# One visit of the attention products instead of two in the gated stage of an mLSTM cell with a SwiGLU block

## The chip, the cores and the metric

The kernel runs on one core of one Trainium2 chip. The metric is the device time of one execution in microseconds (us). The engines are TensorE (PE; its weight loads are shown apart as PEld), VectorE (DVE), ScalarE (ACT), GpSimd (POOL) and SyncE (SP, which here only issues DMA transfers). Each engine works through its own queue in order and waits for the others by semaphores.

## The reference

Two blocks follow one another. The first is an mLSTM cell over 4 batches, 8 heads, 768 positions and 40 features per head (float32): a decaying matrix state per head, with exponential gates, a normaliser and an output gate.

```python
m_new = np.maximum(f_gate[:, :, t] + m, i_gate[:, :, t])
f_stab, i_stab = np.exp(f_gate[:, :, t] + m - m_new), np.exp(i_gate[:, :, t] - m_new)
C = f_stab * C + i_stab * outer(v_t, k_t)        # (40 x 40) per head
n = f_stab * n + i_stab * k_t
y_t = sigmoid(o_gate_t) * (C @ q_t) / max(|n . q_t|, 1)
```

The result, as a matrix x of 3072 tokens by 320 features, goes through `(silu(x @ w_gate) * (x @ w_val)) @ w_out` with an inner width of 1536. The output is 3072 by 320.

## The kernel before, in words

The 768 positions are cut into six groups of 128 (`NG`), and each group into two halves of 64. The cell is computed group by group in the form of attention: within a half, scores of q and k (`sp`) times weights from the gates (`w_sb`) times v, and from the state at the start of the half, q times the state `C`. The 32 heads of all batches are dealt with in two sets P = 0 and 1 of 16 heads each.

The feed-forward block works on one group (512 tokens) at a time: `hidden` and `project_all` for group 0, and for the groups g = 1 to 5 the stage `gated` (products with w_gate and w_val) and then `project_seven` (product with w_out). While group g is in `gated`, the cell of the next group n = g + 1 is computed in between, and the data of group f = g + 2 is loaded. So attention products stand in the gated stages of g = 1 to 4.

`gated` runs over k = 0 to 5. In each step TensorE computes, on PSUM tiles `gv_x` (X) and `gv_y` (Y), two banks each: the first products of X (copied by ACT, L932, into a room `uw` in `tmp` or `x_sb`), the last product of the step before into its Y (`second(k-1)`), the first products of Y, and the second products of X, which are added to the same PSUM tile as the first. DVE adds Y to the room (L942), and X to a second room `c12` (L951); ACT takes the Silu of X (L950) and of `c12` (L952), DVE (L953) and POOL (L955) multiply. `second` is followed by L920 on DVE, L922 on ACT, L923 and the sums L790 to L792 on POOL.

Four places in each step are called "a" (after the first products of X), "b" (after `second`), "c" (after the first products of Y) and "d" (at the end). The dictionary `at`, filled near the end of the file, says by hand which functions are called at which place and step; their instructions enter each engine's queue in exactly that order. Nothing is reordered afterwards. The PSUM of this part is a list `pairs` of four pairs of banks: `take` removes the pair at the front, `give` and `pairs.append` put one back at the end, and the first write to a pair waits for what read it before.

The attention of one set P consists of: `attend_inter` (L433, q times the state) and `attend_intra` (L442, weights times v), 32 products each on TensorE, which the profile shows as 64 records; `gather` on DVE, which multiplies the first by the decay (L451, twice), adds the second (L455, four times), and makes the divisor `den` (L458 to L460); `gate` on POOL (L465), which multiplies the output gate `o_sb` by `den`; and `divide` on DVE (L471, twice), which writes x into the space of `k_sb` (`x_all`). From there `send_squares` (L484) moves x in blocks of 32 by 32 into `x_sq`, where `turn_inputs` (L488, on DVE, in `project_seven`) reads it. `loads_behind` issues the transfers of v (L139) and of the weights (L515) for group f, which overwrite what the intra products read.

Of the kernel before, what the change touches and what calls it, by code (L numbers as in the profile page):

```python
# [24 lines left out]
def kernel(  # L25
# [18 lines left out]
    nc = tc.nc  # L44
    B, H, S, D = q.shape
    BH = B * H
    NG = S // L
# [5 lines left out]
    DM, DF = moe_w_gate.shape  # L53
# [3 lines left out]
    SQ = 32  # L57
    NKC = DM // HP
# [35 lines left out]
    def give(name, P):  # L94
        if held:
            pairs.append(held[name].pop(0))

    def half(i):
        return slice(i * SUB, (i + 1) * SUB)
# [5 lines left out]
    def heads(P):  # L105
        return slice(P * UH, (P + 1) * UH)
# [6 lines left out]
    vw_sb = const.tile([128, BH, D1], F32)  # L113
# [14 lines left out]
    x_sq = const.tile([128, B * NKC, L // SQ, SQ], F32)  # L128
# [168 lines left out]
    for u in range(B):  # L297
        r = slice(u * BH, (u + 1) * BH)
        for P in range(2):
            a = u * BH + P * UH + u * HQ  # L300
# [142 lines left out]
                                 start=True, stop=True)  # L443
        return intra

    def gather(n, P, inter, intra):
        y = vw_sb[:, heads(P)]
        y2 = y.rearrange("p (a two) d -> p two a d", two=2)
        e2 = e_T[:, n, heads(P)].rearrange("p (a two) -> p two a", two=2)
        for two in range(2):  # L450
            nc.vector.tensor_tensor(y2[:, two], inter[two], e2[:, two].unsqueeze(2).to_broadcast([128, UA, D1]), op=ALU.mult)  # L451
        give("inter", P)
        for i, c in QUAD:
            t = y2[half(i), i ^ c]
            nc.vector.tensor_tensor(t, t, intra[i][half(c)], op=ALU.add)  # L455
        give("intra", P)
        den = work.tile([128, UH, 1], F32, name="den")
        nc.vector.scalar_tensor_tensor(den, in0=y[:, :, D:], scalar=-1.0, in1=y[:, :, D:], op0=ALU.mult, op1=ALU.max)  # L458
        nc.vector.tensor_scalar(den, den, scalar1=1.0, scalar2=None, op0=ALU.max)
        nc.vector.reciprocal(den, den)  # L460
        return y, den
# [15 lines left out]

    x_all = k_sb.rearrange("p h d -> p (h d)")[:, 0:B * DM]

    def send_squares(P):  # L480
        for t in range(L // SQ):
            src = x_all[t * SQ:(t + 1) * SQ, 2 * P * DM:(2 * P + 2) * DM].rearrange("p (w e) -> p w e", e=2 * SQ)
            for r in range(2):
                nc.sync.dma_start(out=x_sq[r * SQ:(r + 1) * SQ, 2 * P * NKC:(2 * P + 2) * NKC, t, :],  # L484
                                  in_=src[:, :, r * SQ:(r + 1) * SQ])

    def turn_inputs(n, u):
        nc.vector.transpose(out=xT(n)[half(0), :, ts(u, L)],  # L488
# [470 lines left out]
    live = {}  # L959
# [8 lines left out]
    def do_add(n, pairs_of=(0, 1)):  # L968
        for P in pairs_of:
            live["add", P] = add(n, P)  # L970
# [18 lines left out]
    def do_intra(P):  # L989
        live["intra", P] = attend_intra(P)  # L990

    def do_attend(n, P):
        do_inter(n, P)
        do_intra(P)

    def do_gather(n, P, then=True):
        live["y", P] = gather(n, P, live.pop(("inter", P)), live.pop(("intra", P)))
        if then:
            do_gate(P)

    def do_gate(P):
        gate(P, live["y", P][1], nc.gpsimd)
# [4 lines left out]
    def load_all(dst, a, n, eng=nc.sync):  # L1007
        for P in range(2):
            load(dst, a, n, P, eng)

    run = lambda f, *a, **b: (lambda: f(*a, **b))
# [15 lines left out]
        9: [run(do_weigh, 0), run(do_weigh, 1), run(do_decayed, 2)],  # L1027
        10: [run(do_add, 1, (0,)), run(rounded, 12), run(load_squares, q_sq, q, 2, (0,))],
        11: [run(do_intra, 0), run(do_inter, 1, 0), run(do_gather, 1, 0, False), run(piece_load, 10),
             run(load_squares, q_sq, q, 2, (1,))],  # L1030
    }
# [7 lines left out]
    def early_squares(part):  # L1039
# [7 lines left out]
    after = {  # L1047
        0: [run(do_inter, 1, 1), run(convert, 14), run(sig, 0), run(sig, 1), run(do_gate, 0)],
        1: [run(do_intra, 1), run(do_gather, 1, 1), run(weights_load, 2), run(load_all, v_sb, v, 2), run(load_all, k_sb, k, 2)],
        2: [run(do_divide, 1, 0), run(convert, 15), run(early_squares, 0)],  # L1050
        3: [run(do_divide, 1, 1), run(weights_cap, 0)],
# [20 lines left out]
    def loads_behind(f):  # L1072
        return [run(load_all, v_sb, v, f), run(weights_load, f)]

    def between(g):
        n, f = g + 1, g + 2
        at = {i: [] for i in range(8)}
        if f < NG:
            at[0] += [run(load_squares, q_sq, q, f)]
        if n < NG:  # L1080
            at[0] += [run(turn_inputs, n, u) for u in range(B)]
            at[1] += [run(double_inputs, n, u) for u in range(2)]
        if f < NG:
            at[2] += [run(weights_cap, 0), run(weights_cap, 1)]
            if g == 1:
                at[1] = [run(out_weights, V, 2)] + at[1]
            at[3] += [run(weights_bias, f, 0), run(weigh_values, G, 0), run(weights_bias, f, 1), run(weigh_values, G, 1)]
            at[4] += [run(sig, 0), run(sig, 1), run(turn_squares, q_sq, qT)]
        if n < NG:
            at[4] += [run(input_sums, V)]  # L1090
        if f < NG:
            at[6] += [run(do_decayed, 2 * f)]
        return at

    for g in range(1, NG):
        n, f = g + 1, g + 2
        at = {}
        if n < NG:
            at["a", 0] = []
            if g > 1:  # L1100
                do_add(n)
                at["a", 0] = [run(do_state, 2 * n)]
            at["b", 1] = [run(do_scores), run(do_weigh, 0), run(do_weigh, 1)]
            at["b", 2] = [run(do_attend, n, 0), run(do_gather, n, 0)]
            at["d", 2] = [run(do_divide, n, 0), run(send_squares, 0)]
            at["b", 3] = [run(do_attend, n, 1), run(do_gather, n, 1)]
            at["d", 3] = [run(do_divide, n, 1), run(send_squares, 1)]
        if f < NG:
            at["a", 0] += [run(load_squares, k_sq, k, f)] + ([run(load_all, o_sb, o_gate, 2)] if g == 1 else [])
            at["c", 1] = [run(turn_squares, k_sq, kT)]  # L1110
            at["b", 3] += loads_behind(f)
            at["d", 3] += [run(load_all, o_sb, o_gate, f)]
            at["b", 4] = [run(load_all, k_sb, k, f)]
        if g == 1:
            at["b", 4] = at.get(("b", 4), []) + [run(out_weights, V, 0)]
            at["d", 4] = [run(out_weights, V, 3)]
            at["c", 5] = [run(out_weights, V, 1)]
            at["b", 2] = [run(sig, 0), run(sig, 1)] + at["b", 2]
            for j, w, e, parts in ((1, ("b", 0), G, (0, 1)), (2, ("c", 0), G, (0, 1)), (3, ("d", 0), V, (0,)), (3, ("c", 1), V, (1,)),
                                   (4, ("c", 2), G, (0, 1)), (5, ("a", 4), V, (0, 1))):  # L1120
                at[w] = [run(weight_sums, j, e, parts)] + at.get(w, [])
        gated(g, at)
        project_seven(g, between(g))
# [30 lines left out]
```

## Time and profile before

| what | value |
|---|---|
| median of 3 runs | 517.11 us (509.97, 519.29, 517.11) |
| the profiled execution | 509.04 us, span 507.2 us |
| granted TensorE clock | 1.000 |
| TensorE busy | 501.3 us, 99% of the span |
| DVE, ACT, POOL busy | 332.8, 208.2, 260.2 us |
| gated stages g = 1 to 4, with attention | 53.5 us each (from 123.2, 201.1, 279.0 and 357.0 us) |
| gated stage g = 5, without attention | 46.8 us (from 433.5 us) |
| inter products L433, all | 640 records, 11.7 us |
| intra products L442, all | 640 records, 11.3 us |
| x_sq<-k_sb transfers | 64 of 40 KB, 3.0 us to landing |

The page gives for each group of instructions the line of the kernel, the engine, the operation, the tiles written and read, the busy time, the mean of one instruction and the idle time of the engine ahead of it. The chain that ended last is followed back from the last instruction, at each step to what released it. A timeline has the start and the length of merged instructions of one engine in order; in brackets stands how long the engine was idle before and what released it. Matmuls overlap in the pipeline, so the difference of two starts says more about the cost of a block than the length of one record.

### The profile page before, as it was taken

Reading aid. Unit: us, or ns where it says so; the run is one execution under the profiler, and the core shown is the slowest. Engines: PE = TensorE matmul, PEld = TensorE weight load, DVE = VectorE, ACT = ScalarE, POOL = GpSimd, SP = SyncE. Lnnn points to the kernel's source line nnn. Section 1 sums busy time; section 2 is a strip of 40 time slices with the busy share of each in tenths; the row PEclk is TensorE's granted clock in tenths of the full one; section 3 lists DMA queues with packets and bytes.
Section 4 is the critical chain, followed back from the end, with each engine's and each line's share of the span. In section 5 each row is a group of like instructions: output and inputs, shape, how many; then the busy total and the mean of one; then the engine's idle time right before and its main releaser. Section 6 shows DMA issues by size and latency. Waiting matters only on the chain.

```text
span 507.2 us, 15081 instructions
## 1 busy us (share of the span) xinstructions
PE 501.3 (99%) x6437; PEld 425.8 (84%) x6437; DVE 332.8 (66%) x543; ACT 208.2 (41%) x404; POOL 260.2 (51%) x292
## 2 busy tenths in 40 slices
PE   8999999999999999999999999999999999999997
PEld 4855555767998899888899888899888899988896
DVE  5889668889998677578375677477568454233421
ACT  3675774467252356323248312339321330223200
POOL 3744433358877834466634357643357650176710
PEclk9999999999999999999999999999999999999999
DMA  9999998696705991403992503991101100000001
GB/s 147 190 250 224 170 225 181 142 178 109 105 5 89 164 92 55 55 1 61 172 107 41 74 3 52 163 126 20 42 3 25 31 2 27 27 1 1 0 14 39
DMA packets 184746, 43.29 MB, mean 85 GB/s; under 512 B 173000, under 2 KB 180184, under 8 KB 184040
## 3 DMA queue, kind: packets, MB, share of 16 engines
q1 hardware_dynamic: 183284, 38.26, 47.6%
q0 software_dynamic: 1264, 4.02, 3.2%
q8 instruction: 50, 0.82, 0.7%
q14 instruction: 16, 0.13, 0.1%
q10 hardware_dynamic: 132, 0.07, 0.0%
HBM read 35.68 MB, written 4.01 MB: 78 GB/s over the span
## 4 chain that ended last, share of the span: by engine, by line
PE 92%; DMA 3%; SPq 2%; ACT 1%; DVE 1%; issue 0%; DVEq 0%; ACTq 0%
PE gv_x L902 26%; PE o_ps L823 23%; PE gv_y L902 21%; PE o_ps L769 5%; PE gv_ps L752 5%; PE inter L433 2%; PE sp L384 2%; DMA raw<-in_moe_w_val_dram 2%; PE intra L442 2%; PE add L410 2%; DMA M_dram<-M_sb 1%; SPq L139 1%; ACT h_sb L583 1%; PE sp L600 1%; PE burn L546 1%; PE tp_x L507 1%
## 5 line engine op out<-in xcount | busy, mean ns | idle before, releaser
L902 PE MATMUL gv_x<-xT,wgv_sb 64*128 64x256 f32 x720 | 89.1, 377 | 0.0
L902 PEld LDWEIGHTS gv_x<-xT,wgv_sb 64*128 64x128 f32 x720 | 69.6, 187 | 7.9 <-issue 0.2
L823 PE MATMUL o_ps<-wo_sb,h_sb 128*128 128x160 f32 x480 | 67.4, 300 | 0.0
L823 PEld LDWEIGHTS o_ps<-wo_sb,h_sb 128*128 128x128 f32 x480 | 65.6, 190 | 1.7 <-issue 1.7
L950 ACT ACTIVATE h_sb<-gv_x 128x256 f32<-128x256 f32 x30 | 11.5, 383 | 116.3 <-PE gv_x L902 116.3
L752 PE MATMUL gv_ps<-xT,wgv_sb 64*128 64x512 f32 x240 | 53.7, 595 | 0.1
L752 PEld LDWEIGHTS gv_ps<-xT,wgv_sb 64*128 64x128 f32 x240 | 25.6, 187 | 23.1 <-issue 20.3
L902 PE MATMUL gv_y<-xT,wgv_sb 64*128 64x256 f32 x360 | 43.9, 376 | 0.0
L902 PE MATMUL gv_y<-q_sb,wgv_sb 64*128 64x256 f32 x360 | 43.9, 376 | 0.0
L395 POOL TENSOR_TENSOR vw_sb<-v_sb,w_sb 128x656 f32<-128x656 f32 x10 | 13.9, 1389 | 49.9 <-ACT w_sb L534 38.1
L902 PEld LDWEIGHTS gv_y<-xT,wgv_sb 64*128 64x128 f32 x360 | 35.0, 187 | 3.9
L902 PEld LDWEIGHTS gv_y<-q_sb,wgv_sb 64*128 64x128 f32 x360 | 35.0, 187 | 3.9
L823 PE MATMUL o_ps<-wT,S 128*128 128x160 f32 x240 | 33.4, 299 | 0.0
L823 PEld LDWEIGHTS o_ps<-wT,S 128*128 128x128 f32 x240 | 32.9, 190 | 0.0
L534 ACT ACTIVATE w_sb<-w_sb,g_T 128x64 f32<-128x64 f32 x128 | 31.0, 336 | 0.0
L902 PE MATMUL gv_x<-q_sb,sw 64*128 64x256 f32 x240 | 30.9, 376 | 0.0
L943 POOL TENSOR_TENSOR tmp<-tmp 128x512 f32<-128x512 f32 x15 | 20.0, 1332 | 16.8 <-DVE tmp L942 16.8
L923 POOL TENSOR_TENSOR h_sb<-x_sb 128x512 f32<-128x512 f32 x12 | 15.7, 1311 | 24.6 <-ACT x_sb L922 24.6
L923 POOL TENSOR_TENSOR h_sb<-tmp 128x512 f32<-128x512 f32 x13 | 16.5, 1269 | 21.5 <-ACT tmp L922 21.5
L769 PE MATMUL o_ps<-wo_sb,h_sb 128*128 128x320 f32 x96 | 27.4, 439 | 0.0
L790 POOL TENSOR_TENSOR S<-h_sb 128x256 f32<-128x256 f32 x30 | 22.6, 754 | 9.2 <-DVE h_sb L923 7.3
L942 DVE TENSOR_TENSOR tmp<-tmp,gv_y 128x1024 f32<-128x1024 f32 x15 | 18.1, 1205 | 13.8 <-PE gv_y L902 12.0
(226 smaller groups left out, 993.4 us busy)
## 6 DMA issues: line engine op xcount, KB each, us to landing
w_sb<-M_dram SPq DMA_DIRECT2D x10, 512.0 KB, 6.7
v_sb<-in_v_dram SPq DMA_DIRECT2D x12, 320.0 KB, 6.2
o_sb<-in_o_gate_dram SPq DMA_DIRECT2D x12, 320.0 KB, 5.9
raw<-in_moe_w_out_dram SPq DMA_DIRECT2D x3, 1280.0 KB, 7.1
k_sb<-in_k_dram SPq DMA_DIRECT2D x10, 320.0 KB, 7.6
x_sq<-k_sb SPq DMA_DIRECT2D x64, 40.0 KB, 3.0
q_sb<-in_q_dram SPq DMA_DIRECT2D x32, 64.0 KB, 3.7
raw<-in_moe_w_gate_dram SPq DMA_DIRECT2D x3, 640.0 KB
```

Source lines behind the costliest of these rows:

```text
L384: nc.tensor.matmul(sp[two][half(i), a, :], lhsT=kT[feats(two), P * UA + a, half(i)], rhs=qT[feats(two), P * UA + a, half(i)], start=True, ...
L395: eng.tensor_tensor(vw_sb[:, heads(P)], v_sb[:, heads(P)], w_sb[:, heads(P), last].to_broadcast([128, UH, D1]), op=ALU.mult)
L534: nc.scalar.activation(w_sb[:, h], w_sb[:, h], AF.Exp, bias=g_T[:, n, h:h + 1], scale=-1.0)
L752: nc.tensor.matmul(ps[i], lhsT=wgv_sb[half(i), m, kc, :], rhs=x[half(i), kc, :], start=(kc == 0), stop=(kc == NKC - 1))
L769: nc.tensor.matmul(ps[u], lhsT=hid(g, m)[:, ts(u, L)], rhs=wo_sb[:, m, :], start=(m == 0), stop=(m == NFC - 1))
L790: eng.tensor_tensor(S1[:, k], lo[:, second_half], hi[:, second_half], op=ALU.add)
L823: nc.tensor.matmul(node[x][:, i], lhsT=lhs(k)[:, ts(i, L)], rhs=rhs(k), start=start and k == 0 and i == 0, stop=stop and k == KH - 1, skip ...
L902: nc.tensor.matmul(ps[:, i, cols], lhsT=lhs(c)[half(i)], rhs=rhs(c)[half(i)], start=start and c == 0, stop=stop and c == n - 1, skip_group ...
L923: (nc.vector if k == KH - 1 else nc.gpsimd).tensor_tensor(h_sb[:, 2 * k + 1], uw[:, 0], uw[:, 1], op=ALU.mult)
L942: nc.vector.tensor_tensor(uw, uw, y, op=ALU.add)
L943: nc.gpsimd.tensor_tensor(uw[:, :, second_half], uw[:, :, second_half], uw[:, :, first_half], op=ALU.add)
L950: nc.scalar.activation(h[:, first_half], x[:, 0, first_half], AF.Silu)
```

## The change

Before, the inter and intra products of set 0 stood at place "b" of k = 2, and those of set 1 at place "b" of k = 3, each followed by its gather on DVE; set 0 was divided and sent at "d" of k = 2, set 1 at "d" of k = 3. Now the inter products of both sets and then the intra products of both follow one another at "b" of k = 2. The first part of `gather`, the multiplication by the decay, is a function of its own (`scaled`) and is called for both sets between the inter and the intra products, and gives their PSUM pairs back. Gather 0 follows at "b" of k = 2, gather 1 and divide 0 at "c" of k = 2, divide 1 at "d" of k = 2. After it `send_squares` moves both sets in one series: 8 transfers of 80 KB instead of 16 of 40 KB. `loads_behind` moves from "b" of k = 3 to "d" of k = 2, ahead of divide 1 and the transfers. On POOL the gate of set 1 now stands ahead of L955 and the sums of k = 2. Each engine issues the same computing instructions as before.

```diff
-    def gather(n, P, inter, intra):
+    def scaled(n, P, inter):
...
+    def gather(n, P, intra):
...
-    def send_squares(P):
+    def send_squares():
         for t in range(L // SQ):
-            src = x_all[t * SQ:(t + 1) * SQ, 2 * P * DM:(2 * P + 2) * DM].rearrange("p (w e) -> p w e", e=2 * SQ)
+            src = x_all[t * SQ:(t + 1) * SQ].rearrange("p (w e) -> p w e", e=2 * SQ)
             for r in range(2):
-                nc.sync.dma_start(out=x_sq[r * SQ:(r + 1) * SQ, 2 * P * NKC:(2 * P + 2) * NKC, t, :],
-                                  in_=src[:, :, r * SQ:(r + 1) * SQ])
+                nc.sync.dma_start(out=x_sq[r * SQ:(r + 1) * SQ, :, t, :], in_=src[:, :, r * SQ:(r + 1) * SQ])
...
+    def do_scaled(n, P):
+        scaled(n, P, live.pop(("inter", P)))
...
-            at["b", 2] = [run(do_attend, n, 0), run(do_gather, n, 0)]
-            at["d", 2] = [run(do_divide, n, 0), run(send_squares, 0)]
-            at["b", 3] = [run(do_attend, n, 1), run(do_gather, n, 1)]
-            at["d", 3] = [run(do_divide, n, 1), run(send_squares, 1)]
+            at["b", 2] = [run(do_inter, n, 0), run(do_inter, n, 1), run(do_scaled, n, 0), run(do_scaled, n, 1),
+                          run(do_intra, 0), run(do_intra, 1), run(do_gather, n, 0)]
+            at["c", 2] = [run(do_gather, n, 1), run(do_divide, n, 0)]
+            at["d", 2] = (loads_behind(f) if f < NG else []) + [run(do_divide, n, 1), run(send_squares)]
+            at["d", 3] = []
...
-            at["b", 3] += loads_behind(f)
```

More of the change, by code (lines that the diff above doesn't have):

```diff
@@ L444, in attend_intra @@
         return intra
-    def gather(n, P, inter, intra):
-        y = vw_sb[:, heads(P)]
-        y2 = y.rearrange("p (a two) d -> p two a d", two=2)
+    def scaled(n, P, inter):
+        y2 = vw_sb[:, heads(P)].rearrange("p (a two) d -> p two a d", two=2)
         e2 = e_T[:, n, heads(P)].rearrange("p (a two) -> p two a", two=2)
@@ L452, in gather @@
         give("inter", P)
+    def gather(n, P, intra):
+        y = vw_sb[:, heads(P)]
+        y2 = y.rearrange("p (a two) d -> p two a d", two=2)
         for i, c in QUAD:
@@ L994, in do_attend @@
         do_intra(P)
+    def do_scaled(n, P):
+        scaled(n, P, live.pop(("inter", P)))
     def do_gather(n, P, then=True):
-        live["y", P] = gather(n, P, live.pop(("inter", P)), live.pop(("intra", P)))
+        if ("inter", P) in live:
+            do_scaled(n, P)
+        live["y", P] = gather(n, P, live.pop(("intra", P)))
         if then:
```

## The prediction

> **What bounds the kernel now.** I read the page from the top (busy shares, then the chain that ended last), then the chain in order of time for one stage, then the timeline of each engine in that stretch.
>
> ```profile
> PE 501.3 (99%) x6437; PEld 425.8 (84%) x6437; DVE 332.8 (66%) x543; ACT 208.2 (41%) x404; POOL 260.2 (51%) x292
> ...
> PE 92%; DMA 3%; SPq 2%; ACT 1%; DVE 1%; issue 0%; DVEq 0%; ACTq 0%
> ```
>
> TensorE works all the time and is 92% of the chain; nearly all of the other 8% lies before 90 us, where the change does nothing. The chain in the stage g=2, around both visits of the attention products:
>
> ```profile
> 219.59 1.29 PE gv_y L902 x12
> 220.89 1.07 PE inter L433 x64
> 221.96 0.93 PE intra L442 x64
> 222.90 2.36 PE gv_y L902 x20
> 225.25 4.32 PE gv_x L902 x40
> ...
> 239.55 3.45 PE gv_y L902 x32
> 243.00 4.32 PE gv_x L902 x40
> ```
>
> Every piece starts where the one before ends: no engine makes TensorE wait here, and the stages g=1, 3 and 4 look the same. So only two things can move the end: TensorE's own work, and a new wait of TensorE. DVE (33 to 46 us busy of each 53.5 us stage) has slack on average; what counts is where its queue is late.
>
> **The change, part by part.** Let T be the start of the first inter product, by the timeline 220.82 us in g=2 (142.93, 298.72 and 376.70 in the others).
>
> *TensorE.* A half-step without attention is 3.45 of gv_y; with a visit it is 1.29 + 1.07 + 0.93 + 2.36 = 5.65, so a visit costs 2.20 us. By the starts in the timeline that is 0.95 from inter to intra, 0.95 for intra, and about 0.30 for the changes of kind (gv_y's twelve take 1.40 instead of 1.29 up to inter, intra takes 1.05 up to gv_y, the next eight 0.97 instead of 0.87). The same 256 records are issued per stage, but one visit goes. Two visits are 4.40; one long one is 4 x 0.95 + 0.30 = 4.10. **Gain 0.30 us per stage, 1.2 us in four stages** (0.8 to 1.4: two inter blocks in a row are not in this trace; the bounds are 0.2 and 0.35 by the two ways of reading the changes).
>
> *New wait for PSUM.* The pool has four pairs and X of k=2 holds one. inter 0, inter 1 and intra 0 take the other three, so intra 1 gets inter 0's pair and must wait for the two DVE multiplications that now stand first, and the next gv_y gets inter 1's. Inter 0 ends about T+1.1; L451 starts at T+1.21 (222.03) and two take 0.91, so that pair is free at T+2.12, and intra 1 wants it at T+2.85. The second pair is free at T+3.07 (two more, 0.93 apart), and gv_y wants it at T+3.90. Both have 0.7 to 0.8 us to spare, in g=1 too, where DVE came late from its transposes and still began L451 at T+1.21 (144.14). Cost nothing; each us that DVE is later than T+1.9 would cost one.
>
> *New order on DVE.* This is the step that I expect to cost. Gather 1 and divide 0 used to stand in the next half-step; now they stand ahead of L951 of k=2. Behind L951 stands, on ACT, the Silu L952, and behind that the copy L932 of k=3's first products, which TensorE must see finished before it adds the second products to the same pair. The rows of before:
>
> ```profile
> 222.03 0.91 DVE L451 TENSOR_TENSOR vw_sb<-inter,e_T 128x328 f32<-128x328 f32 x2 [0.35 <-PE inter L433]
> 222.96 2.02 DVE L455 TENSOR_TENSOR vw_sb<-vw_sb,intra 64x328 f32<-64x328 f32 x4
> 225.01 0.33 DVE L458 SCALAR_TENSOR_TENSOR den<-vw_sb 128x16 f32<-128x16 f32 x1
> ...
> 226.22 1.16 DVE L942 TENSOR_TENSOR x_sb<-x_sb,gv_y 128x1024 f32<-128x1024 f32 x1
> 228.31 0.69 DVE L951 TENSOR_TENSOR x_sb<-x_sb,gv_x 128x512 f32<-128x512 f32 x1 [0.92 <-ACT h_sb L950]
> ...
> 229.24 1.44 DVE L471 TENSOR_TENSOR k_sb<-o_sb,vw_sb 128x320 f32<-128x320 f32 x2
> ```
> ```profile
> 229.03 0.42 ACT L952 ACTIVATE x_sb<-x_sb 128x256 f32<-128x256 f32 x1 [0.76 <-DVE x_sb L951]
> 229.67 1.01 ACT L932 COPY tmp<-gv_x 128x1024 f32<-128x1024 f32 x1 [0.23 <-PE gv_x L902]
> 231.69 0.63 ACT L922 ACTIVATE x_sb<-x_sb 128x512 f32<-128x512 f32 x1 [1.01 <-DVE x_sb L920]
> ```
>
> In before that copy ends at 230.68 and TensorE needs it at 235.06 (second gv_x products of k=3): 4.4 us of cover. After, DVE goes: four L451 to T+3.07; four additions of gather 0 (intra 0 lands about T+3.1) 2.05, to T+5.17; den 1.21, to T+6.38; L942 waits for gv_y (T+3.90+0.97+1.30, and 0.26 until it is seen) and starts at T+6.43, 1.14 to T+7.57; gather 1 2.05 + 1.21, to T+10.83; divide 0, d; then 0.72 from L951 to L952, 0.33 from L952 to the copy (219.49 to 219.81 in k=1), 1.00 of copy, 0.06 to be seen. The copy is done at T+12.94+d. TensorE arrives at the second products at 235.06 - 220.82 - 0.30 = T+13.94. **Stall = d - 1.0.** L471's single durations run from 484 to 1039 ns, so d for two lies between 0.9 and 2.1. In before the pair took 1.44 beside 0.81 us of Pool. Now it begins together with Pool's gate 1 (L465, 1262 ns): 0.9 free, plus 0.54 x 1.26/0.81 = 0.84, gives d = 1.75, near the upper rows; in g=1 Pool's weight sums lie there instead, and the pair beside them took 1.80. Stall 0.75 per stage, 3.0 in four; the ends are 0 and 1.1.
>
> [...]
>
> What is late next: divide 1 follows L953 and ends by T+15.4, L920 of k=2 by T+16.1, L942 of k=3 by T+17.3; TensorE asks for these at T+19 or later, so they stay covered, by about 2 us. Pool reaches L943 of k=3 some 3 us later than now, which delays a DVE instruction and no product.
>
> *Transfers.* Sixteen sends of 40 KB (a batch of eight keeps SP's queue 6.5 to 7.9 us, 3.0 us to landing) become eight of 80 KB, and the loads of v and w move ahead of them, from T+17 to T+4 or so. One new send takes between one old issue (0.84) and two; eight take 7 to 14 us from T+15.4, so they are issued by g=2's 243 to 250, against 249.05 now. Their reader, L488, runs at 257.01. Behind them the loads of o and k come no later, and those of q, free only when gv_y's last use of q_sb ends at 254.66, begin at 255.57 now and at most 0.9 earlier. Gain and loss nothing: everything lies under TensorE.
>
> **Sum.** 4 x (0.75 - 0.30) = **+1.8 us** on the profiled execution (span 507.2, time 509.04): 510.8. The ends are -1.2 (no stall) and +3.6 (stall 1.1, gain 0.2). The other three executions shown took 509.97, 517.11 and 519.29, on which a change of this size is lost; the mean of the four is 513.85, and with 1.8 I forecast **515.7 us**, 1.4 below the median of the runs with nothing added.
>
> **Rivals.**
> 1. No stall: DVE finishes divide 0 within 1.0 us, as the shortest L471 rows would have it, and only the saved visit is left: -1.2 us, 512.7. For it: TensorE waited for nothing in the stages; against it: Pool's gate starts in the same moment.
> 2. Slower by over 2%, through the same place: TensorE stands in k=3 before its second gv_x products because the copy is late. Price: each us beyond d = 1.0 costs 4 us over the stages, and 2% (10.2 us) is passed at d = 3.85, that is, if the DVE and ACT chain of 10.6 us from T+2.2 ran about a fifth longer than its rows. A stall of 2.85 in each stage gives 524.1 on the mean. For it: the whole 4.4 us of cover is spent and nothing is left to absorb a miss; against: the chain's rows repeat within 0.1 us in three stages.
> 3. The transfers don't do what they seem to: 640 short rows of one send land so late that L488 waits. They would have to land after 257, some 7 to 14 us after their issue, against 3.0 (at most 7.4) now; a delay of 3 us per stage shifts TensorE only when input sums come after 279, and they end at 274.7. Time as forecast, 516.
>
> **How the numbers follow.** Forecast with a stall 0.55; no stall 0.25; slower through the stall 0.10; transfers 0.02; the rest, 0.08, is scatter between executions, since 509 to 519 is itself 2%, and 2% is about what a measurement of this kernel can tell from no change. I split it 0.05 faster, 0.03 slower. Faster 0.05, same 0.82, slower 0.13. Range: 509.04 - 1.2 = 507.8 to 519.29 + 3.6 = 522.9, so 508 to 523; it leaves out the second rival and some scatter.
>
> **What would show it.** In the profile after: inter x128 and intra x128 in one block per stage, some 4.1 us long with its changes; no idle time before intra; L932 of k=3 ending near T+14.7, and TensorE idle 0.4 to 1.1 us before the second gv_x products of k=3, released by ACT. Wrong if TensorE waits instead before intra 1 or gv_y (the PSUM pairs), if the wait in k=3 is over 2 us, or if L488 waits for a transfer.

## The result and the profile after

| what | before | after |
|---|---|---|
| median, 22 runs each, side by side | 511.19 us (508.91 to 520.17) | 518.53 us (513.91 to 526.58) |
| ratio | | 1.0121, 95% interval 1.0098 to 1.0143 |
| the profiled execution, span | 509.04 us, 507.2 | 518.4 us, 516.6 |
| start of the state products (`add`, L410) of groups 1 to 4 | 121.66, 199.71, 277.60, 355.50 | 123.86, 206.30, 285.81, 364.76 |
| from one to the next (g=1, g=2, g=3) | 78.05, 77.89, 77.90 | 82.44, 79.51, 78.95 |
| from the fourth to the end of the span (g=4, g=5) | 151.70 | 151.84 |

The kernel got 1.2% slower, 6.2 us, where +1.8 was forecast. The ratio leaves out the slow executions (five of after's 22, from 522.54 us up), so it lies below the ratio of the two medians, which are 7.3 us apart. Lines of the new kernel have slightly higher numbers in what follows: the copy L932 is L934, L942 is L944, L951 to L955 are L953 to L957, L465 is L468 and L471 is L474. The last three rows of the table cut the span at a point that every kernel of this study has; a period holds one gated stage and the product with w_out behind it. The spans differ by 9.4 us: 2.20 before group 1, where the change does nothing (that stretch varies from execution to execution, as the table of the experiments shows), then 4.39, 1.62 and 1.05 in the stages g=1, 2 and 3, and 0.14 in all that follows.

The page's busy shares and the shares of the chain, after:

```profile
PE 505.1 (98%) x6437; PEld 426.6 (83%) x6437; DVE 335.9 (65%) x543; ACT 208.1 (40%) x404; POOL 266.3 (52%) x292
...
PE 87%; DVE 4%; DMA 3%; ACT 2%; issue 2%; SPq 1%; DVEq 0%; ACTq 0%
```

The number of products is the same, TensorE's busy time grew by 3.8 us only, and its share of the chain fell from 92 to 87%. "issue", time in which an engine waited for nothing that the profile shows, rose from 0 to 2% of the chain. The chain of the stage g=2 in order of time (start, length, what) shows where:

```profile
226.18 1.29 PE gv_y L904 x12
227.47 2.01 PE inter L433 x128
229.48 1.28 PE intra L442 x87
230.75 1.43 issue
232.18 0.83 PE intra L442 x41
233.01 2.36 PE gv_y L904 x20
...
243.16 4.59 PE gv_x L904 x40
```

In the middle of the intra products TensorE stands still for 1.43 us. No engine releases it, and the place is not record 64, where the products of the second set, with inputs and a PSUM pair of their own, begin: it is record 87 of 128. The other stages have the same, at other places (timeline of TensorE; in brackets the idle time before the piece and its releaser):

```profile
147.30 1.10 PE L442 MATMUL intra<-v_sb,w_sb 64*64 64x41 f32 x58
150.19 1.93 PE L442 MATMUL intra<-v_sb,w_sb 64*64 64x41 f32 x70 [1.78 <-issue]
...
308.80 1.93 PE L442 MATMUL intra<-v_sb,w_sb 64*64 64x41 f32 x116
311.55 0.43 PE L442 MATMUL intra<-v_sb,w_sb 64*64 64x41 f32 x12 [0.82 <-issue]
...
387.85 2.33 PE L442 MATMUL intra<-v_sb,w_sb 64*64 64x41 f32 x128
```

The idle time lies behind record 58, 87 and 116 of intra in g=1, 2 and 3, each time 29 records further. In g=4 nothing is cut off, but 128 records that otherwise take 2.08 take 2.33. Before has no idle time in any of its eight visits of 64 + 64 records.

Two smaller things appear besides. In the last row of the chain the second products of X in k=3 take 4.59 instead of 4.32: that is the forecast wait for the copy, and it comes back below. And the windows of g=1 (length, busy time and number of instructions of each engine, then the granted clock, the DMA share and GB/s) show a slow clock:

```profile
144.90:150.10 5.20, 3.24 (x188) 2.96 (x186) 3.58 (x8) 4.14 (x6) 2.83 (x4) 1.00 0.02 5
150.50:153.90 3.40, 3.40 (x73) 2.99 (x69) 2.59 (x7) 1.26 (x1) 1.42 (x3) 0.50 0.56 98
154.00:163.00 9.00, 9.00 (x86) 7.74 (x82) 7.12 (x13) 1.10 (x3) 6.74 (x8) 1.00 0.73 156
```

Right behind the 1.78 us of idle time TensorE had half its clock for 3.4 us, which costs 1.7 us of work. With it g=1 adds up: 1.78 idle, 1.7 clock, 0.50 before the copy, 0.27 before the second inter block, less 0.30 for the saved visit, is 3.95 of 4.39 (1.7 is an estimate, half of 3.4).

### The profile page after: what moved, and what is told of

Its sections match the earlier page's. It is cut to its first block, busy times and chain, and to the rows that moved or that the text cites. A ratio compares the mean times of both kernels' runs of the same rounds, so it can differ in the third digit from the quotient of the medians.

```text
span 516.6 us, 15035 instructions
## 1 busy us (share of the span) xinstructions
PE 505.1 (98%) x6437; PEld 426.6 (83%) x6437; DVE 335.9 (65%) x543; ACT 208.1 (40%) x404; POOL 266.3 (52%) x292
## 4 chain that ended last, share of the span: by engine, by line
PE 87%; DVE 4%; DMA 3%; ACT 2%; issue 2%; SPq 1%; DVEq 0%; ACTq 0%
PE gv_x L904 23%; PE o_ps L825 22%; PE gv_y L904 19%; PE gv_ps L754 7%; PE o_ps L771 5%; DMA raw<-in_moe_w_gate_dram 3%; PE intra L442 2%; PE inter L433 2%; PE add L410 2%; PE sp L384 1%; ACT h_sb L585 1%; DMA o_sb<-in_o_gate_dram 1%; SPq L368 1%; PE tp_x L509 1%; PE sp L602 1%
## 5 line engine op out<-in xcount | busy, mean ns | idle before, releaser
L944 DVE TENSOR_TENSOR tmp<-tmp,gv_y 128x1024 f32<-128x1024 f32 x15 | 18.3, 1219 | 16.8 <-PE gv_y L904 15.1
L904 PE MATMUL gv_y<-q_sb,sw 64*128 64x256 f32 x200 | 27.5, 395 | 0.0
L792 POOL TENSOR_TENSOR S<-h_sb 128x256 f32<-128x256 f32 x30 | 22.6, 755 | 9.3 <-DVE h_sb L925 7.3
L944 DVE TENSOR_TENSOR x_sb<-x_sb,gv_y 128x1024 f32<-128x1024 f32 x15 | 18.3, 1219 | 13.7 <-PE gv_y L904 12.0
```

The costliest lines, as they stand in the source:

```text
L792: eng.tensor_tensor(S1[:, k], lo[:, second_half], hi[:, second_half], op=ALU.add)
L904: nc.tensor.matmul(ps[:, i, cols], lhsT=lhs(c)[half(i)], rhs=rhs(c)[half(i)], start=start and c == 0, stop=stop and c == n - 1, skip_group ...
L944: nc.vector.tensor_tensor(uw, uw, y, op=ALU.add)
```

## The theories

**A, the instruction stream.** By this theory TensorE's instructions come in pieces that a transfer brings. The profile shows two queues of the kind "instruction", one of 16 packets and this one:

```profile
q8 instruction: 51, 0.84, 0.7%
```

51 packets of 0.84 MB are 16 KB each (50 and 0.82 before). TensorE has 6437 products and as many weight loads, 12,874 records, or 257 per packet of before; so a piece is estimated at some 256 instructions, 128 product records. In a block of inter and intra a piece is used up in 1.9 us (128 records at 0.95 us per 64); among the products gv_x and gv_y, at 0.108 us each, it would last some 14 us. A visit of before is 128 records, no more than one piece; the long block is 256, two pieces within 3.9 us. By the theory the second has to be waited for if it takes longer than 1.9 us to arrive. The transfers in a window of 0.2 us at the moment concerned in g=2 (packets, MB, share of 16 engines' time):

```profile
q8 instruction: 1, 0.02, 44.7%
```

This is the window from 229.3 to 229.5, and it holds one packet, with 1.43 us of one DMA engine. The products resume at 232.18, 2.7 to 2.9 us later. In the trace this packet runs from 229.40 to 230.83, so TensorE goes on 1.35 us after its end; in g=1 and 3 the packets end at 148.80 and 310.27, 1.39 and 1.28 us ahead of the products. The same holds in all kernels of this study: of the pauses on "issue" that the timelines of TensorE show from 60 us on, 33 end 1.23 to 1.61 us after the end of such a packet and 2.2 to 3.0 us after its start, and one, of 0.21 us in e4_sends_only, does not. The size of a piece is borne out by e5_twice, whose 1024 further products bring 8 further packets (58 against 50), 128 products for each. And the step of 29 records fits: a whole period has 1123 products by the windows of before (201.1 to 279.0 us and 279.0 to 356.9), which is 9 pieces of 128 less 29, so from stage to stage the piece ends fall 29 records further into the block: 58, 87, 116, and 145, that is 17 of the piece after.

**B, the loads.** `loads_behind` moved from k=3 to a place some 13 us earlier, so transfers now begin near the block; they might hold up TensorE or its instructions.

**C, the copy.** The forecast wait before the second products of X in k=3; by it a later gather 1 and divide 0 give the time back.

## The experiments

All ratios are to before, executed again on the same chip as each set of runs, with their 95% interval; e1 to e4, e5 to e8 and e9 are three such sets. The periods are those of the table above, from one `add` to the next.

| kernel | ratio | first `add` | period g=1 | g=2 | g=3 |
|---|---|---|---|---|---|
| before | 1 | 121.66 | 78.05 | 77.89 | 77.90 |
| after | 1.0121 (1.0098 to 1.0143) | 123.86 | 82.44 | 79.51 | 78.95 |
| e8_again, the changed kernel once more | 1.0107 (1.0052 to 1.0163) | 125.03 | 79.75 | 79.64 | 79.54 |
| e1_loads_late | 1.0075 (1.0036 to 1.0115) | 123.01 | 80.46 | 79.33 | 79.25 |
| e2_phase | 1.0204 (1.0137 to 1.0271) | 128.81 | 80.16 | 78.85 | 79.43 |
| e3_gather_late | 1.0060 (1.0032 to 1.0089) | 121.91 | 83.05 | 78.58 | 78.68 |
| e4_sends_only | 0.9978 (0.9947 to 1.0010) | 124.54 | 78.31 | 77.88 | 77.89 |
| e5_twice | 1.0474 (1.0418 to 1.0530) | 123.50 | 84.32 | 83.24 | 85.37 |
| e6_pad | 1.0168 (1.0124 to 1.0211) | 123.93 | 80.85 | 79.92 | 79.91 |
| e7_split | 1.0066 (1.0024 to 1.0107) | 128.95 | 79.31 | 77.89 | 77.90 |
| e9_two_blocks | 0.9996 (0.9966 to 1.0025) | 128.12 | 78.53 | 77.93 | 78.09 |

### Loads back to their place (e1_loads_late)

```diff
-            at["d", 2] = (loads_behind(f) if f < NG else []) + [run(do_divide, n, 1), run(send_squares)]
+            at["d", 2] = [run(do_divide, n, 1), run(send_squares)]
+            at["b", 3] = loads_behind(f) if f < NG else []
```

> The changed kernel with the loads of v and of the weights put back to place b of k=3. Theory A (instructions): the idle time of TensorE inside the intra products of the changed kernel (1.78, 1.43, 0.82 us in g=1, 2, 3 and nearly none in g=4) comes from TensorE's own instruction stream, which is fetched in pieces of 16 KB; a block of 256 small records uses pieces up faster than they arrive (2.2 to 2.8 us from the start of a fetch to the next product). Then the idle times stay, 0.8 to 1.8 us at the same records, and the ratio to the kernel before stays at 1.009 to 1.015. Theory B (transfers): the loads, which in the changed kernel are issued just when the first intra products end and are missing in g=4, hold the fetch up. Then the idle times are under 0.3 us and the ratio falls to at most 1.004.

The idle times stay, at the same records (timeline of TensorE, g=1 and g=2):

```profile
148.94 1.27 PE L442 MATMUL intra<-v_sb,w_sb 64*64 64x41 f32 x70 [1.41 <-issue]
...
229.18 0.83 PE L442 MATMUL intra<-v_sb,w_sb 64*64 64x41 f32 x41 [1.24 <-issue]
```

In g=3 it is 0.92 behind record 116, in g=4 0.37 behind record 18. B falls: the first of these transfers is now issued at 167.08 in g=1, long after the block. Whether e1 is faster than the changed kernel at all is open: 1.0075 lies inside e8_again's interval, and the intervals of e1 and after overlap. It also lies just under the 1.009 to 1.015 that theory A was given; the places and sizes of the idle times, not the ratio, tell A from B.

### Other piece ends (e2_phase)

```diff
-    fill("add", 18, False)
+    fill("add", 18 + 64, False)
```

64 more products with no effect on the output stand at the start of the program, so every later instruction is 64 records further in its piece.

> The changed kernel with 64 more idle products on dummy data (bfloat16, 18 become 82) at the beginning, which moves every later instruction of TensorE by 128 places, half of a 16 KB piece. They take about 46 ns each, 2.9 us in all, ahead of a wait for weights that may hide a part. Theory A: the idle times follow the places where pieces end, 64 records earlier: g=4, which had nearly none, gets 1.2 to 1.8 us; g=3 goes up to 1.2 to 1.8; g=1 or g=2 loses most of its 1.4 to 1.8. Theory B: the idle times stay at records 58, 87 and 116 of the intra products of g=1, 2 and 3, and g=4 keeps none.

The timeline of TensorE in the four stages:

```profile
152.26 1.98 PE L442 MATMUL intra<-v_sb,w_sb 64*64 64x41 f32 x121
155.39 0.32 PE L442 MATMUL intra<-v_sb,w_sb 64*64 64x41 f32 x7 [1.15 <-issue]
...
231.96 0.53 PE L442 MATMUL intra<-v_sb,w_sb 64*64 64x41 f32 x23
233.30 1.73 PE L442 MATMUL intra<-v_sb,w_sb 64*64 64x41 f32 x105 [0.81 <-issue]
...
310.81 0.99 PE L442 MATMUL intra<-v_sb,w_sb 64*64 64x41 f32 x53
313.10 1.36 PE L442 MATMUL intra<-v_sb,w_sb 64*64 64x41 f32 x75 [1.30 <-issue]
...
390.25 1.45 PE L442 MATMUL intra<-v_sb,w_sb 64*64 64x41 f32 x82
392.79 0.90 PE L442 MATMUL intra<-v_sb,w_sb 64*64 64x41 f32 x46 [1.09 <-issue]
```

This settles the place. 58, 87, 116 and 17 (in g=4, where e1 and e3 show it behind 18 and 20) plus 64, less 128 where it passes that, are 122, 23, 52 and 81; measured 121, 23, 53 and 82. The work, the data and the other engines are the same at all of these places; only the position in the instruction stream is not. The stage g=4, which had next to nothing, now has 1.09 us. The sizes were not as expected: g=4 stays under 1.2 us, and neither g=1 nor g=2 loses most of its idle time (1.15 and 0.81).

The kernel as a whole is the slowest but one for a reason outside the stages: the 64 products themselves, and in the profile TensorE also stands 1.76 us, again on "issue", behind record 107 of the `sp` block at 75 us, with half the clock for 6.8 us behind that. In that stretch the DMA engines are loaded to the full (share 1.21 by the windows from 70 to 76 us); whether this delayed the fetch was not tried.

### Gather 1 and divide 0 behind the multiplications of X (e3_gather_late)

```diff
-            at["c", 2] = [run(do_gather, n, 1), run(do_divide, n, 0)]
-            at["d", 2] = (loads_behind(f) if f < NG else []) + [run(do_divide, n, 1), run(send_squares)]
+            at["c", 2] = []
+            at["d", 2] = ([run(do_gather, n, 1), run(do_divide, n, 0)] + (loads_behind(f) if f < NG else [])
+                          + [run(do_divide, n, 1), run(send_squares)])
```

> The changed kernel with gather 1 and divide 0 put behind the two DVE instructions that end k=2. The idle time of TensorE ahead of the second gv_x products of k=3 (0.50 us in g=1, 0.2 to 0.3 with the slow restart in g=2 to 4) goes, as the copy of k=3 no longer stands behind them; by theories A and B alike the idle times inside intra stay. About 1.2 us less than the changed kernel, ratio 1.007 to 1.013. If the wait for the copy were the main cost of the change, the ratio would fall to under 1.004.

The wait for the copy is gone and the idle times inside intra stay (1.62, 0.82, 0.83 and 0.46). The period g=3 gives the copy's price: with 0.83 us of idle time, as after's 0.82, it is 78.68 instead of 78.95, so C is worth 0.27 us in a stage. The ratio came out just under its range, and some 3 us below after's where the four copy waits (0.50 and three of 0.27) make 1.3; what the rest is, is open, and e8_again's interval holds both ratios. In g=1 half the clock lasted 6.8 us, from 147.6 to 154.4, and that is the 83.05.

### The transfers alone (e4_sends_only)

```diff
-            at["d", 2] = [run(do_divide, n, 0), run(send_squares, 0)]
+            at["d", 2] = [run(do_divide, n, 0)]
-            at["d", 3] = [run(do_divide, n, 1), run(send_squares, 1)]
+            at["d", 3] = [run(do_divide, n, 1), run(send_squares)]
```

This is before, with the eight sends of 80 KB behind divide 1.

> The kernel before with the sends of x alone changed: eight of 80 KB after divide 1 at place d of k=3 in place of two series of eight of 40 KB. If the transfers are covered, as predicted: ratio 0.997 to 1.003, and no new idle time of TensorE. If the larger sends land late, DVE waits for them at its transposes and the ratio is over 1.005.

0.9978 with an interval that holds 1, and periods that agree with before within 0.01 in g=2 and g=3: the eight transfers cost nothing and bring nothing at this place. (In g=1 there is 0.21 us on "issue" between inter and intra, at 147.00; no instruction packet goes with it.) With the earlier place and the loads ahead of them, as in the change, they stand in e9_two_blocks below.

### Long blocks without the change (e5_twice)

```diff
-        for a in range(UA):
+        for a in [x for _ in range(2 if n > 1 else 1) for x in range(UA)]:
```

Before, with the inter and, in the same way, the intra products of each visit in the gated stages issued twice into the same tiles: blocks of 256 records in the old order of DVE and the transfers, twice per stage.

> The kernel before with the inter and the intra products of each visit in the gated stages issued twice (the second time they overwrite the same PSUM with the same values), so that each of its eight visits is a block of 256 small records like the one of the changed kernel, while the loads, the transfers and the order on DVE stay as before. Added work alone: 8 x 1.9 = 15.2 us, ratio 1.030. Theory A: most of the eight visits get idle times of 0.5 to 1.8 us inside them, 6 to 10 us in all, ratio 1.040 to 1.052. If the changed kernel's idle times came from its loads, its order on DVE or its PSUM pairs, none appear here and the ratio is 1.027 to 1.033.

Seven of the eight visits have an idle time inside intra. The waits of the whole execution (total us, times, longest) have it in one line, which before doesn't have:

```profile
PE intra L442 <- issue: 8.6, 7, 1.6
```

In the first visits it comes behind records 58, 88, 119 and 21, after's places to within four records, as it must if a stage has 256 more records (two whole pieces) than before it. So the length of the block suffices. The ratio itself says little, as twice the products cost their own time.

### Eight products between inter and intra (e6_pad)

```diff
-                          run(do_intra, 0), run(do_intra, 1), run(do_gather, n, 0)]
+                          run(do_intra, 0, 8), run(do_intra, 1), run(do_gather, n, 0)]
```

The 8 is a number of products of gv's shape (64 x 256 columns, 16 records in the profile) that intra 0 writes into its own PSUM pair first and then overwrites. They break the block into 128 + 128 records with 1.93 us between.

> The changed kernel with eight dummy products of the gated kind (16 records of 108 ns, 1.73 us) between the inter and the intra products of each stage; they write the PSUM pair that intra 0 overwrites, so nothing else changes. Theory A: a piece of 256 instructions then lasts about 3.4 us instead of 1.9, longer than a fetch, so the idle times inside intra fall to at most 0.3 us; the time is that of the changed kernel plus 4 x 1.9 for the dummy products minus about 4 for the idle times that go: ratio 1.015 to 1.020. If the idle times came from the intra products themselves (their operands, their PSUM pairs), they would stay and the ratio would be 1.023 to 1.028.

No idle time inside intra (L447 in this kernel) in any of the four stages; g=1 is shown:

```profile
147.51 2.00 PE L441 MATMUL intra<-xT,wgv_sb 64*128 64x256 f32 x16
149.44 2.08 PE L447 MATMUL intra<-v_sb,w_sb 64*64 64x41 f32 x128
```

The products that buy this cost more than they save, 4 x 1.93 us. The periods of 79.92 and 79.91 are 2.0 over before: 1.93 for the products, less 0.30, plus 0.28 for the copy, is 1.91.

### Three quarters of the block (e7_split)

```diff
-                          run(do_intra, 0), run(do_intra, 1), run(do_gather, n, 0)]
-            at["c", 2] = [run(do_gather, n, 1), run(do_divide, n, 0)]
+                          run(do_intra, 0), run(do_gather, n, 0)]
+            at["c", 2] = [run(do_intra, 1), run(do_gather, n, 1), run(do_divide, n, 0)]
```

> The changed kernel with intra 1 moved from place b to place c of k=2, behind the first gv_y products, so that the block is 192 records and a second of 64. Theory A, with pieces ending every 128 records, at records 58, 87, 116 and 17 of the block in g=1 to 4 and again 128 later: the second end lies inside the block only in g=1 (186) and g=4 (145). So g=1 keeps 1 to 1.8 us, g=4 0 to 0.5, and g=2 and g=3, which had 1.4 and 0.8, lose theirs. Two visits again, so no gain of 0.3 us per stage. Ratio 1.002 to 1.008. If block length is not what counts, g=2 and g=3 keep idle times.

```profile
152.40 1.10 PE L442 MATMUL intra<-v_sb,w_sb 64*64 64x41 f32 x58
154.17 0.32 PE L442 MATMUL intra<-v_sb,w_sb 64*64 64x41 f32 x6 [0.67 <-issue]
...
231.26 1.12 PE L442 MATMUL intra<-v_sb,w_sb 64*64 64x41 f32 x64
```

With 192 records the piece end falls into the block only in g=1 (record 58 of 64) and, in g=4, behind 17 records, where intra's 64 take 1.52 instead of 1.12. In g=2 and g=3 the end would come behind 87 and 116 records, which this block no longer has; there the periods are before's, 77.89 and 77.90. Of the 3.4 us that the ratio makes, the stages explain 1.26 (g=1, with 0.28 before the second inter block) and some 0.4 (g=4). Expected for g=1 was 1 to 1.8 of idle time; it is 0.67. The profiled execution, 2.8 us over the median of this kernel, has more ahead of the stages: 2.62 us on "issue" at 97.96 and half the clock for 3.4 us from 86.09; how much of this the other executions have isn't known.

### Two blocks of one piece (e9_two_blocks)

```diff
-                          run(do_intra, 0), run(do_intra, 1), run(do_gather, n, 0)]
-            at["c", 2] = [run(do_gather, n, 1), run(do_divide, n, 0)]
-            at["d", 2] = (loads_behind(f) if f < NG else []) + [run(do_divide, n, 1), run(send_squares)]
+            at["c", 2] = [run(do_intra, 0), run(do_intra, 1), run(do_gather, n, 0)]
+            at["d", 2] = ([run(do_gather, n, 1), run(do_divide, n, 0)] + (loads_behind(f) if f < NG else [])
+                          + [run(do_divide, n, 1), run(send_squares)])
```

Both inter blocks stay at "b" of k=2, both intra blocks come at "c", and gather 1 and divide 0 stand as in e3. The change is kept otherwise, earlier loads and eight transfers included.

> The changed kernel with its block cut in two: the inter products of both sets stay at place b of k=2, the intra products of both and gather 0 go to place c, behind the first gv_y products; gather 1 and divide 0 stand behind the two DVE instructions that end k=2. The eight sends, the earlier loads and the order of everything else stay as changed. If the block of 256 records and the wait for the copy are the whole cost of the change, none of the idle times is left (at most 0.3 us anywhere in the four stages), each stage takes 53.3 to 53.7 us, and the ratio to the kernel before is 0.997 to 1.003. If something else of the change costs, the ratio stays over 1.004.

0.9996 (0.9966 to 1.0025): all that the change lost is back, and nothing is won. The windows of the stages g=1 and g=2, in the columns of above (g=3 and g=4 are 53.66 and 53.55 long, and as busy as g=2):

```profile
129.90:183.54 53.64, 53.38 (x817) 47.20 (x813) 46.89 (x70) 18.27 (x27) 40.26 (x44) 1.00 0.65 99
...
208.17:261.63 53.46, 53.46 (x817) 47.36 (x817) 33.90 (x58) 14.67 (x24) 31.43 (x35) 1.00 0.57 88
```

TensorE is busy in all of three stages and in all but 0.26 us of g=1. The stages take 214.31 us together, before's 213.88: two visits again, one of inter and one of intra.

Ahead of the stages, though, this execution has one large pause of the same kind (timeline of TensorE):

```profile
97.14 0.55 PE L433 MATMUL inter<-C,qT 40*64 40x41 f32 x21 [2.32 <-issue]
```

It lies in a block of only 64 intra and 64 inter records, behind eight long products. e7 has 2.62 and e1 0.94 us at the same record; in before nothing is cut off there, but the 64 inter records take 1.51 instead of 1.14. In e9 the packet ran from 94.61 to 95.64, in before from 87.89 to 89.08, ahead of the inter block (89.43). So a short block is no guarantee where the packet starts late. The DMA engines were loaded (share 0.86 from 92 to 98 us in e9); whether that delayed it was not tried.

### The changed kernel once more (e8_again)

> The changed kernel once more, beside the next three on the same chip. Theory A: idle inside intra again at records 58, 87 and 116 of g=1, 2, 3, and 0.1 to 0.5 us in g=4, with lengths that differ by some tenths of a us between executions, as a fetch takes 0.9 to 1.6 us; ratio 1.006 to 1.014. If the granted clock shows a half-speed stretch, it follows an idle time of over 1.5 us.

1.0107, and idle times of 0.67, 1.55, 0.95 and 0.19 at the same records 58, 87, 116 and 18. No half clock shows this time, and the four stages are 5.66 us longer than before's, against 5.5 by the ratio. Of these the separate idle times are 3.36; the copy's 0.49 in g=1 and 0.27 in the other stages, 0.27 before the second inter block in g=1, and the saved visits, -1.2, add 0.37. The blocks take another 1.27 beyond 4.10 and their idle times (why, see below), and 0.45 stand in g=3 ahead of the block, where the stretch from the first gv_x to `sp` takes 10.15 instead of 9.70. The last 0.2 were not assigned. No pause here is followed by half the clock, so the last sentence of the expectation was not put to the test.

## Why the prediction was wrong

**The step that failed is the cost on TensorE of the moved products.** The prediction added the visit's parts (0.95 per 64 records and 0.30 for the changes) and got a block of 4.10 us, a gain, and it said that only TensorE's own work and a wait for another engine could move the end. It left out a third thing, the arrival of TensorE's instructions, which the row "q8 instruction" named in the profile of before. Its own list of what would prove it right had "no idle time before intra"; there are 0.7 to 1.8 us inside intra in g=1 to 3. A (e2: the place follows the instruction stream; e5: the long block alone suffices; e6 and e9: blocks of one piece have none in the four stages; and the pauses end 1.23 to 1.61 us behind a packet) stands. What fills the time from a packet's end to the next product, and why a packet starts when it does, is not resolved.

**The saved visit is real, but a pause eats more than its idle time.** By the prediction's measure (the time from the first products of Y before the block to the gv_x behind it, beyond a half-step's 3.45) two visits of before take 4.42. The block of after takes 4.35 in g=4, or 4.10, as worked out, without the 0.25 by which its intra products are stretched. In g=2 and g=3 it takes 5.75 and 5.20, and without the idle times still 4.32 and 4.38: products that follow one another overlap (64 inter records last 1.14, and the next block starts 0.95 after their start), and across a pause they don't, so that a pause costs some 0.2 to 0.3 more than the idle time shows. With that the period of g=3 adds up: 5.20 - 4.42 is 0.78, and 0.27 for the copy makes 1.05. So the gain of 0.30 stood against 0.8 to 1.8 us of idle time and 0.2 to 0.3 beside it.

**The copy wait was right in place and mechanism, too big by the divisor's rows.** TensorE does wait before the second gv_x of k=3, for ACT's L934. The rows of g=4 (T = 385.96):

```profile
395.83 0.19 DVE L461 SCALAR_TENSOR_TENSOR den<-vw_sb 128x16 f32<-128x16 f32 x1
...
396.43 1.89 DVE L474 TENSOR_TENSOR k_sb<-o_sb,vw_sb 128x320 f32<-128x320 f32 x2
398.24 0.68 DVE L953 TENSOR_TENSOR x_sb<-x_sb,gv_x 128x512 f32<-128x512 f32 x1
```
```profile
399.27 1.00 ACT L934 COPY tmp<-gv_x 128x1024 f32<-128x1024 f32 x1
```

d was 1.81 from L474's start to L953's, against 1.75. But `den` took 0.60 from its first start to L474, not 1.21: in before these three ran beside POOL's L790 to L792 (the second took 0.64 there), here POOL was idle (0.17). The other way went L944, which began at T+6.69 instead of T+6.43. So the copy ended at T+14.31, 0.06 before it is seen, where T+14.69 was forecast for its being seen, against an arrival of T+14.18 (400.14), not T+13.94, because the block itself had got longer. The stall is 0.27 with the restart (0.50 in g=1, where the profile names L934 as the releaser), not 0.75. That d came out near 1.75 is in part luck: the prediction stretched the pair in proportion to POOL's time, but the first L474 took 0.43, and the second, begun at 396.78 beside gate 1 (POOL L468, 396.59 to 397.97), took 1.54, where the shortest single row of before has 0.48, and ended 0.35 after the gate.

**What cost nothing, as forecast.** In g=2 to 4 TensorE waits for no PSUM pair between the first inter product and gv_y; e6 and e9, where no idle time inside intra could cover such a wait, show none either. In g=1 there is one that the prediction had not, 0.27 us before the second inter block, on a pair of X. The profile names ACT's L954 as the releaser; by the program the pair's last reader is DVE's L955, which came late behind the transposes (L374, to 145.33) and ended at 146.23, against the block's start at 146.38. e1, e2 and e6 to e9 have it too, e3 and e5 have not. The transfers cost nothing (e4); the eight sends are issued between 243.47 and 248.87 in g=2, at T+16, in 5.40 us, less than the 7 to 14 allowed for.

**The sum and the base.** Forecast +1.8 us, measured 5.5 (e8_again) to 6.2 us. The 515.7 stood on a mean of four executions, 513.85; 22 executions have a median of 511.19. So it lay below the 517.11 shown and pointed the other way from the +1.8 that it contained. That 518.53 is only 2.8 above 515.7 is luck: a base that was 2.7 too high made up for part of an effect that was 3.7 to 4.4 too small (5.5 by the medians). The rival "slower through the copy wait" reached 2% by more of the same stall; the time instead came from a place that no rival named.

## What to carry to other kernels

Count small matmuls in a row: where 256 records of 0.95 us per 64 followed one another, twice as many as an instruction packet is estimated to hold, TensorE stood still inside the block for 0.19 to 1.78 us with no engine releasing it, and the profile calls that "issue". Putting the blocks of small products together saved 0.30 us per stage at the seams here and cost 0.67 to 1.78 us of idle time in g=1 to 3 of after and e8_again. In e6 and e9, where products of 0.108 us each stand between blocks of 128 records, the gated stages have no such idle time, so alternate the two kinds. Even 128 records stood still for 2.3 us in e9, ahead of the stages, where the packet ran from 94.61 to 95.64 and the block began at 93.00. When a wait lies inside a run of identical instructions and no engine releases it, see whether its place moves with dummy instructions put in far ahead.

## What the hardware showed beyond that

**How long a piece end holds TensorE up varies.** It was 0.19 to 1.78 us for 256 records in one block; the smallest, 0.19 to 0.46, came in g=4 behind record 18 or 20 (after, e8, e1, e3), but e5's g=4 has 0.94 behind record 21. As every pause ends 1.23 to 1.61 us behind its packet, the size goes with when the packet starts and how long it takes (0.88 to 1.55): in g=4 of e8 and e1 it starts 0.21 and 0.06 us ahead of the first inter product, in g=1 of the same kernels 1.38 and 2.33 behind it. Why it starts then is open.

**Half the clock after a short pause.** In after and e3, g=1, the granted clock was 0.50 for 3.4 and 6.8 us around the end of a pause of 1.78 and 1.62 us, and e2 had 6.8 us of it at a pause of 1.76 us at 75 us. e7 and e9 had 3.4 us of it behind a wait for DVE of 1.93 and 1.91 us, at 82 to 84 us. But the same wait in e8_again, 1.93, and pauses of 1.55 and 1.60 in e5, 2.62 in e7 and 2.32 in e9 brought none, so the length of the pause alone doesn't decide. The clock records of after's trace begin at 7.16 (1.00), 150.52 (0.50), 153.94 (1.00) and 515.75 us (0.50), that is 42, 1 and 106 times 3.413 us apart. What brings the half clock on was not shown. By these rows such a pause can cost another 1.7 to 3.4 us, an estimate from half the clock over 3.4 and 6.8 us. This may be part of why after's runs spread over 513.9 to 526.6 us; that was not measured.
